# Attention then experts: the first expert's w2 is split on ScalarE and VectorE, piece by piece among the last weighted sums, instead of on GpSimd

## The chip, the cores and the metric

The kernel runs on one core of a Trainium2 chip. The metric is device time in microseconds, from runs of the whole program; lower is better. The core has a matrix engine (TensorE, PE in the rows, PEld for its weight loads), VectorE (DVE), ScalarE (ACT), GpSimd (POOL) and SyncE (SP), which here only issues DMAs. Each engine works through its own instructions in order and waits on semaphores for the others.

## The reference

Attention over 4 batches of 8 heads with a hash mask, and then a mixture of 8 experts, one expert for each token:

```
mask   = q_bucket[:, :, :, None] == k_bucket[:, :, None, :]
scores = where(mask, scale * q @ k.T, -1e9);  attn = softmax(scores);  attn_out = attn @ v
x      = attn_out as (3072, 512)
e_idx  = argmax(x @ w_gate);  gate_w = softmax(...)[e_idx];  eom = sigmoid(x @ w_output_gate)
out[mask_e] = gate_w * eom * (relu(x[mask_e] @ w1[e]) @ w2[e])
```

Sizes: sequence 768, head 64, model width 512, expert width 1024. Everything is float32.

## The kernel before

**Attention.** Heads are taken in 16 pairs, in steps of one 128-row tile. A step makes scores on PE, takes the minimum on DVE (line 534), the exponential on ACT (542), scales on GpSimd (552), transposes on PE with copies on ACT (563, 564), and adds the weighted sum over v on PE (`weighted`, 574). When half of a pair is summed (`c == NT - 1`), DVE copies it to the tile `ot` (577); `rows` transposes it (586) and SP writes it to x_dram (593).

**Routing.** For each batch, small matmuls and some twenty small DVE instructions choose the expert of every token, its rank there and its gate (lines 603 to 710). For the last batch the last pair's part comes in two halves, `add_pair(0)` and `add_pair(1)`: three small matmuls (628) that read `ot`, and one DVE addition (629). Then `best`, `choose`, `prefix`, `gates`, `ranks`, `cols`, `hot`, `table` and `entries` follow.

**The first expert begins early.** The biggest expert is known one batch before the end. Its first 256 tokens are gathered and its w1 is split while attention still runs. Between the pieces of the last routing `fill(f)` issues one eighth of their first layer: 12 matmuls on PE (312), and a ReLU on ACT (322) that writes `hh`. `low()` issues the DVE instruction that goes with an earlier `fill` (323, writes `hl`) and so gives back the bank of PSUM that it used; there are two such banks, so `fill(k)` needs the `low()` of `fill(k-2)`.

**Splitting weights.** Products of float32 are made of three products of rounded parts. A piece of w2 is 128x1024 numbers, 512 KB: `load_weights` loads it into `w_raw`, `split_weights` makes the rounded part (`w2h`, line 175 on GpSimd or 177 on ACT) and the rest (`w2l`, line 178 on GpSimd or on DVE). The first expert has four pieces, f = 0, 2, 4 and 6. There are two `w_raw` buffers at this time, so the load of piece 4 can start only when both instructions on piece 0 are done, and that of piece 6 when those on piece 2 are.

**What sets the order.** PE, DVE, ACT and GpSimd run in the order in which the code between `with tc.manual_schedule` issues their instructions. SP is not among them: its order comes from the planner of the compiler, which takes a DMA when it takes its inputs and its buffer to be ready. In the kernel before, it puts the loads of w2 ahead of writes to x_dram that stand earlier in the code.

After this stretch come the second layer of the first 256 tokens (`down_rows`, ps_s from w2h, w2l), the order of the experts, and the experts one after another.

Of the kernel before, what the change touches and what calls it, by code (L numbers as in the profile page):

```python
# [46 lines left out]
NFB = F // P  # L47
# [12 lines left out]
def lsh_attention_then_moe(  # L60
# [27 lines left out]
    def signed():  # L88

        for h, s in ((0, 1.0), (1, -1.0)):  # L90
            hs = slice(h * D, (h + 1) * D)
            c = 2 * NB * h
            nc.gpsimd.tensor_scalar(pjc[hs, c:c + NB], pj[hs, 0:NB], s, 0.0, ALU.mult, ALU.add)
            nc.gpsimd.tensor_scalar(pjc[hs, c + NB:c + 2 * NB], pj[hs, 0:NB], -s, 0.0, ALU.mult, ALU.add)
# [64 lines left out]
    def load_weights(shape, src):  # L159
        raws.append(len(raws) % 4 if expert[1:] else len(raws) % 2)  # L160
        if raws[-1] < 2:
            raw = wpool.tile(shape, F32, name="w_raw", bufs=2)
        else:

            raw = f32(gp.tile([P, NCC, CAP0], F32R, name=("xh0", "xlo0")[raws[-1] - 2])).rearrange("p a b -> p (a b)")
            if len(shape) == 3:
                raw = raw.rearrange("p (a b) -> p a b", a=shape[1])
        nc.sync.dma_start(raw, src)
        return raw

    def split_weights(pool, tag, bufs, shape, raw, idle=""):
        hi = pool.tile(shape, F32R, name=tag + "h", bufs=bufs)
        lo = pool.tile(shape, F32R, name=tag + "l", bufs=bufs)
        if "h" in idle:
            nc.gpsimd.tensor_scalar(hi, raw, 1.0, 0.0, ALU.mult, ALU.add)
        else:
            nc.scalar.copy(hi, raw)
        (nc.gpsimd if "l" in idle else nc.vector).tensor_tensor(lo, raw, f32(hi), ALU.subtract)  # L178
        return hi, lo
# [10 lines left out]
    def w2_piece(pool, r, f, idle=""):  # L190
        raw = load_weights([P, 2, DM], w2[bass.ds(expert[r], 1), :, f:f + 2].rearrange("e p f d -> p (e f) d"))
        hi, lo = split_weights(pool, "w2", NFB // 2, [P, 2, DM], raw, idle)
        return [(hi[:, j], lo[:, j]) for j in range(2)]
# [108 lines left out]
    def new_h():  # L302
        return [ep.tile([P, NFB, CAP], F32R, name=n) for n in ("hh", "hl")]
# [64 lines left out]
    with ExitStack() as actx:  # L368
# [20 lines left out]
        def load(g, heads=(0, 1)):  # L389
            st = pairs[g]  # L390
            st.setdefault("qk", [])
            for j in heads:
                t = hp.tile([P, S], F32, name="qk", bufs=4)
                nc.sync.dma_start(t, qkT[2 * g + j])
                st["qk"].append(t)

        def load_v(g):
            pairs[g]["v"] = tp.tile([P, 2, NT, D], F32, name="vt", bufs=2)
            nc.sync.dma_start(pairs[g]["v"], v[g])
# [71 lines left out]
        def first_low():  # L471

            st = pairs[0]
            xl, yl, xr, qk = st["xl"][1], st["yl"][1], st["xr"][1], st["qk"][1]
            for n in range(2):
                cs = slice(n * HS, (n + 1) * HS)
                nc.vector.scalar_tensor_tensor(xr[D:P, cs], qk[D:P, cs], 1.0, f32(xl[D:P, cs]), ALU.mult, ALU.subtract)
                nc.vector.scalar_tensor_tensor(yl[0:D, cs], qk[0:D, cs], -0.125, f32(xl[0:D, cs]), ALU.mult,
                                               ALU.subtract)
            nc.gpsimd.tensor_scalar(xl[D:P], qk[0:D], -0.125, 0.0, ALU.mult, ALU.add)  # L480
# [41 lines left out]
        def scores(s):  # L522
            g, hf, t, j = tile_of(s)
            st = pairs[g]
            qs = slice(t * P, (t + 1) * P)
            ss = ps_s.tile([P, 2, 512], F32, name="ps_s")
            kb = D + 2 * NB
            for l, r, k, first in ((st["xl"][j], st["xr"][j], P, True), (st["yl"][j], st["yr"][j], kb, False)):
                for n in range(2):
                    nc.tensor.matmul(ss[:, n, 0:HS], l[0:k, qs], r[0:k, n * HS:(n + 1) * HS],  # L530
                                     start=first, stop=not first)
            sc = tp.tile([P, 2, HS], F32, name="sc", bufs=LAG + 2)
            mn = sp.tile([P, 1], F32, name="mn")
            nc.vector.tensor_scalar(sc, ss[:, :, 0:HS], MASKED, None, ALU.min, ALU.min, accum_out=mn)  # L534
            return sc, mn
# [10 lines left out]
        def normal(s0):  # L546

            rs = sums.pop(s0 // GROUP)
            nc.vector.tensor_scalar(rs, rs, 1e-9, None, ALU.add)
            nc.vector.reciprocal(rs, rs)  # L550
            for k in range(GROUP):
                nc.gpsimd.tensor_scalar(live[s0 + k], live[s0 + k], rs[:, k:k + 1], 0.0, ALU.mult, ALU.add)  # L552
# [26 lines left out]
        def rows(g, hf, whole=True):  # L579

            b, i = divmod(g, H // 2)
            st = pairs[g]
            if hf == 0:
                st["xb"] = gp.tile([P, S // 32, 32], F32, name="xb", bufs=2)
            ts = slice(hf * HS // 32, (hf + 1) * HS // 32)
            nc.vector.transpose(st["xb"][:, ts].rearrange("p n c -> p (n c)"), st["ot"][:, hf * HS:(hf + 1) * HS])
            if whole:
                if hf == 0:
                    return
                ts = slice(0, S // 32)  # L590
            xv = x_dram[b * S:(b + 1) * S].rearrange("(n r) c -> r n c", r=32)
            for a in range(4):
                nc.sync.dma_start(xv[:, ts, i * P + 32 * a:i * P + 32 * (a + 1)], st["xb"][32 * a:32 * (a + 1), ts])
# [246 lines left out]
        with tc.manual_schedule(engines=MANUAL):  # L840
            load(0)
            load(1)
            load_v(0)
            make_identity(nc, ident)

            warm = ps_t.tile([P, 3, P], F32, name="ps_t")
            for i in range(NWARM):
                nc.tensor.transpose(warm[:, i % 3], ident, ident)
            first_heads()
            live = {}  # L850
            for s0 in range(0, NSTEP + LAG, GROUP):
                for s in range(s0, s0 + GROUP):
                    if s < NSTEP:
                        live[s] = scores(s)
                    if s == 0:
                        first_low()
                        signed()
                    if s == s0 and 0 <= s - GROUP < NSTEP:
                        normal(s - GROUP)
                    if 0 <= s - LAG < NSTEP:  # L860
                        transposed(s - LAG, live.pop(s - LAG))
                    if s < NSTEP:
                        live[s] = soft(s, *live[s])
                    for fn in at.get(s, ()):
                        fn()
                for s in range(s0, s0 + GROUP):
                    for fn in products.get(s, ()):
                        fn()


            hctx.close()
            ep = ctx.enter_context(tc.tile_pool(name="ep", bufs=1, side="right", reuse_waits="tile"))
            hs = new_h()
            w2s = []
            lows = []

            def fill(f):
                lows.append(up(early["w1"], early["x"], hs, [f], CAP0))

            def low():  # L880
                lows.pop(0)()

            fill(0)
            for f in range(0, NFB, 2):
                w2s += w2_piece(ep, 0, f, "hl")
            for c in range(NT):
                weighted(2 * NP - 1, c)
                if c == 0:
                    rows(NP - 1, 0, False)
                if c == 2:  # L890
                    r["add_pair"](0, lp)
            fill(1)
            low()
            r["add_pair"](1, lp)
            fill(2)
            r["best"]()
            low()
            r["choose"]()
            rows(NP - 1, 1, False)
            fill(3)  # L900
            low()
            r["prefix"]()
            fill(4)
            r["gates"]()
            low()
            r["ranks"]()
            fill(5)
            low()
            fill(6)
            r["cols"]()  # L910
            low()
            fill(7)
            r["hot"]()
            r["table"]()
            low()
            r["entries"]()
            gid0 = lead_slots(EARLY)
            low()

    mp = ctx.enter_context(tc.tile_pool(name="mp", bufs=1, reuse_waits="tile"))  # L920
    with tc.manual_schedule(engines=MANUAL):
# [17 lines left out]
        for r in range(E):  # L939
# [3 lines left out]
            if r:  # L943
                hs = new_h()
                w2s = []
# [93 lines left out]
    with tc.If(nr > 0):  # L1039
# [12 lines left out]
        with tc.For_i(0, nr, 1):  # L1052
# [13 lines left out]
            for r in range(E):  # L1066
                more = nc.values_load(left[0:1, r:r + 1], min_val=0, max_val=NTOK)
                with tc.If(more > 0):
                    w1s = [w1_piece(wpool, r, cc) for cc in range(NCC)]
                    w2s = []  # L1070
# [53 lines left out]
```

## Time and profile before

| | |
|---|---|
| time, median of 3 runs | 795.59 us (793.64 to 795.8) |
| profiled execution, its own time | 795.53 us |
| its span, first to last instruction | 793.8 us |
| mean granted TensorE clock | 0.990 |
| busy: PE, DVE, ACT, GpSimd | 771.9, 479.1, 458.6, 381.2 us |

Busy times are averages over stages that have different limits; what a change in one stage is worth is read from that stage. Times in the rows below are in microseconds from the start of the span.

### The profile page before, as it was taken

What the parts mean: (1) busy time and instruction counts of PE and PEld (TensorE: products, weight loads), DVE (VectorE), ACT (ScalarE), POOL (GpSimd) and SP (SyncE); (2) the same over time, 40 slices, a digit from 0 to 9 for tenths busy, and PEclk for the clock granted to TensorE, in tenths of its full rate; (3) what the DMA queues carried; (4) which work ended last, traced back from release to release, by engine and by line L of the source; (5) the groups of instructions that cost most, each with busy time, mean ns of one, the idle gap of its engine ahead of it and who ended that gap; (6) DMA issues with size and microseconds to landing.
All of it is one profiled execution on the core that took longest, in us unless ns stands there. A gap on an engine that the chain in (4) does not pass through costs nothing. (4 is left out here: it accounts for less than half of the span.)

```text
span 793.8 us, 13687 instructions
## 1 busy us (share of the span) xinstructions
PE 771.9 (97%) x4674; PEld 607.3 (77%) x4674; DVE 479.1 (60%) x1034; ACT 458.6 (58%) x934; POOL 381.2 (48%) x422
## 2 busy tenths in 40 slices
PE   7999999999999999999999998989999999998997
PEld 4776776677766767676767667978999999988895
DVE  5776666797766796675896737236262635454540
ACT  5877787777777777777768721233252534442331
POOL 6556544444453444544445883462537364645201
PEclk7999999999999999999999999999999999999999
DMA  4563554464564455455456153353444444535501
GB/s 159 128 149 73 115 126 88 110 140 88 122 146 119 87 130 141 90 123 130 88 124 166 56 134 99 92 198 118 143 148 153 149 146 154 176 122 197 195 24 38
DMA packets 84799, 98.88 MB, mean 125 GB/s; under 512 B 57999, under 2 KB 59439, under 8 KB 84720
## 3 DMA queue, kind: packets, MB, share of 16 engines
q1 hardware_dynamic: 79376, 84.58, 40.7%
q0 software_dynamic: 5200, 13.31, 5.2%
q8 instruction: 39, 0.64, 0.3%
q14 instruction: 40, 0.33, 0.1%
q10 hardware_dynamic: 144, 0.02, 0.0%
HBM read 59.49 MB, written 13.11 MB: 91 GB/s over the span
## 5 line engine op out<-in xcount | busy, mean ns | idle before, releaser
L552 POOL TENSOR_SCALAR sc<-sc,rsum 128x768 f32<-128x768 f32 x192 | 179.0, 944 | 219.2 <-DVE rsum L550 88.6
L534 DVE TENSOR_SCALAR_CACHE_REDUCE sc<-ps_s 128x768 f32<-128x768 f32 x192 | 183.3, 955 | 98.1 <-PE ps_s L530 90.1
L564 ACT COPY pts<-ps_t 128x384 f32<-128x384 f32 x384 | 164.6, 482 | 96.8 <-PE ps_t L563 96.3
L542 ACT ACTIVATE sc<-sc,mn 128x768 f32<-128x768 f32 x192 | 181.5, 945 | 15.9 <-DVE sc L534 15.4
L563 PE MATMUL ps_t<-ident,sc 128*128 128x128 f32 x1152 | 158.4, 273 | 3.7 <-ACT pts L564 1.6
L563 PEld LDWEIGHTS ps_t<-ident,sc 128*128 128x128 f32 x1152 | 137.1, 141 | 14.4 <-POOL sc L552 4.0
L574 PE MATMUL ps_a<-pts,vt 128*64 128x384 f32 x768 | 144.8, 499 | 0.0
L530 PE MATMUL ps_s<-xr,xl 128*128 128x384 f32 x384 | 117.9, 388 | 1.9 <-DVE sc L534 1.8
L530 PEld LDWEIGHTS ps_s<-xr,xl 128*128 128x128 f32 x384 | 58.3, 192 | 72.7 <-issue 33.6
L312 PE MATMUL ps_s<-xh,w1h 128*128 128x256 f32 (+7 forms) x288 | 97.9, 340 | 5.2 <-DVE hl L323 4.0
L530 PE MATMUL ps_s<-yr,yl 76*128 76x384 f32 x384 | 100.9, 344 | 1.5 <-POOL yr L439 1.3
L323 DVE SCALAR_TENSOR_TENSOR hl<-ps_s,hh 128x256 fp32r<-128x256 f32 (+8 forms) x40 | 34.0, 849 | 108.8 <-ACT hh L322 97.2
L312 PE MATMUL ps_s<-xh,w1l 128*128 128x256 f32 (+7 forms) x288 | 96.1, 334 | 0.8 <-DVE w1l L178 0.8
L312 PE MATMUL ps_s<-xlo,w1h 128*128 128x256 f32 (+7 forms) x288 | 95.9, 333 | 0.0
L286 POOL DMA_INDIRECT xq<-x_dram,idx x75 | 81.8, 1091 | 21.6 <-issue 21.1
L329 POOL DMA_INDIRECT out_dram<-yo,sid x29 | 30.6, 1056 | 119.6 <-ACT yo L328 73.0
L574 PEld LDWEIGHTS ps_a<-pts,vt 128*64 128x64 f32 x768 | 46.6, 136 | 50.5 <-issue 47.7
L322 ACT ACTIVATE hh<-ps_s 128x256 fp32r<-128x256 f32 (+8 forms) x40 | 29.1, 727 | 94.6 <-PE ps_s L312 81.4
L530 PEld LDWEIGHTS ps_s<-yr,yl 76*128 76x128 f32 x384 | 70.8, 192 | 2.1 <-POOL yr L439 2.1
L312 PEld LDWEIGHTS ps_s<-xh,w1h 128*128 128x128 f32 x288 | 54.7, 190 | 8.7 <-DVE hl L323 4.8
L312 PEld LDWEIGHTS ps_s<-xh,w1l 128*128 128x128 f32 x288 | 54.6, 190 | 2.6 <-DVE w1l L178 1.6
L312 PEld LDWEIGHTS ps_s<-xlo,w1h 128*128 128x128 f32 x288 | 54.6, 190 | 1.1
(204 smaller groups left out, 1017.7 us busy)
## 6 DMA issues: line engine op xcount, KB each, us to landing
w_raw<-in_w_dram SPq DMA_DIRECT2D x36, 512.0 KB
qk<-in_qkT_dram SPq DMA_DIRECT2D x32, 384.0 KB
xh<-in_w_dram SPq DMA_DIRECT2D x14, 512.0 KB
xlo<-in_w_dram SPq DMA_DIRECT2D x14, 512.0 KB
vt<-in_v_dram SPq DMA_DIRECT2D x16, 384.0 KB
xr<-xl SPq DMA_DIRECT2D x30, 192.0 KB
yr<-xl SPq DMA_DIRECT2D x30, 192.0 KB
xr<-yl SPq DMA_DIRECT2D x30, 192.0 KB
```

The lines of the kernel that those rows point to most:

```text
L286: nc.gpsimd.indirect_dma_start(out=xq[:, k * P:(k + 1) * P], out_offset=None, in_=x_dram.rearrange("n (a f) -> (n a) f", a=NB32), in_offse ...
L312: nc.tensor.matmul(ps, l, r, start=first and k == 0, stop=last and k == len(pairs) - 1)
L322: nc.scalar.activation(hh, ph, AF.Relu)
L323: return lambda: nc.vector.scalar_tensor_tensor(hl, ph, 0.0, f32(hh), ALU.max, ALU.subtract)
L329: nc.gpsimd.indirect_dma_start(out=out[:, :], out_offset=bass.IndirectOffsetOnAxis(ap=sid[0:n, r, a:a + 1], axis=0), in_=yo[0:n], in_offse ...
L530: nc.tensor.matmul(ss[:, n, 0:HS], l[0:k, qs], r[0:k, n * HS:(n + 1) * HS], start=first, stop=not first)
L534: nc.vector.tensor_scalar(sc, ss[:, :, 0:HS], MASKED, None, ALU.min, ALU.min, accum_out=mn)
L542: nc.scalar.activation(pr, pr, AF.Exp, bias=mn, scale=-1.0, accum_out=sums[s // GROUP][:, k:k + 1])
L552: nc.gpsimd.tensor_scalar(live[s0 + k], live[s0 + k], rs[:, k:k + 1], 0.0, ALU.mult, ALU.add)
L563: nc.tensor.transpose(tr[:, c], pr[:, (3 * h + c) * P:(3 * h + c + 1) * P], ident)
L564: nc.scalar.copy(pts[:, 3 * h:3 * h + 3, t * P:(t + 1) * P], tr)
L574: nc.tensor.matmul(st["av"][j * D:(j + 1) * D], st["v"][:, j, c], blocks[hb][j][:, c], start=(c == 0), stop=(c == NT - 1))
```

## The change

The loop that issued all four splits on GpSimd ahead of the last weighted sums is gone. The four pieces are now issued one at a time at four places of the same stretch, and without the argument "hl", so that `split_weights` takes ACT for w2h and DVE for w2l. Piece 0 stands where the loop stood; piece 2 behind the first weighted sum and the `rows` there; piece 4 behind the third and its `add_pair(0)`; piece 6 between `add_pair(1)` and `fill(2)`.

```
             fill(0)
-            for f in range(0, NFB, 2):
-                w2s += w2_piece(ep, 0, f, "hl")
+            w2s += w2_piece(ep, 0, 0)
             for c in range(NT):
                 weighted(2 * NP - 1, c)
                 if c == 0:
                     rows(NP - 1, 0, False)
+                    w2s += w2_piece(ep, 0, 2)
                 if c == 2:
                     r["add_pair"](0, lp)
+                    w2s += w2_piece(ep, 0, 4)
             fill(1)
             low()
             r["add_pair"](1, lp)
+            w2s += w2_piece(ep, 0, 6)
             fill(2)
             r["best"]()
             low()
```

## Rows read from the trace of the kernel before

**Rows 1.** The profile's page: busy times of the engines, and the granted TensorE clock in 40 equal slices of the span, in tenths.

```profile
PE 771.9 (97%) x4674; PEld 607.3 (77%) x4674; DVE 479.1 (60%) x1034; ACT 458.6 (58%) x934; POOL 381.2 (48%) x422
PEclk7999999999999999999999999999999999999999
```

**Rows 2.** Busy time by windows of 1 us beside the last routing: window, its length, busy time of PE, PEld, DVE, ACT and POOL with counts, granted clock, DMA share, GB/s.

```profile
477.00:478.00 1.00, 0.62 (x11) 0.52 (x8) 1.00 (x4) 0.39 (x1) 1.00 (x1) 1.00 0.00 0
479.00:480.00 1.00, 0.21 (x2) 0.02 (x1) 0.93 (x8) 0.38 (x1) 0.00 (x0) 1.00 0.65 94
```

**Rows 3.** Timeline of GpSimd: start, duration, engine and line, what it does; in brackets the idle time before it and what ended it. The four pairs of L175 and L178 are the pieces 0, 2, 4 and 6.

```profile
463.80 2.38 POOL L178 TENSOR_TENSOR w2l<-w_raw,w2h 128x1024 fp32r<-128x1024 f32 x1
...
470.30 1.05 POOL L175 TENSOR_SCALAR w2h<-w_raw 128x1024 fp32r<-128x1024 f32 x1 [0.66 <-PE ps_m L628]
...
475.41 1.05 POOL L175 TENSOR_SCALAR w2h<-w_raw 128x1024 fp32r<-128x1024 f32 x1 [1.59 <-DMA w_raw<-in_w_dram]
476.55 2.44 POOL L178 TENSOR_TENSOR w2l<-w_raw,w2h 128x1024 fp32r<-128x1024 f32 x1
488.27 1.38 POOL L254 DMA_INDIRECT xg<-x_dram,gid  x1 [9.29 <-DVE gid L782]
```

**Rows 4.** Timeline of PE: the last matmul of `fill(1)`, and the first ones of `fill(4)` and `fill(5)`.

```profile
473.24 0.28 PE L312 MATMUL ps_s<-xh,w1l 128*128 128x256 f32 x1
...
477.58 0.39 PE L312 MATMUL ps_s<-xh,w1h 128*128 128x256 f32 x1 [0.38 <-DVE hl L323]
...
480.31 0.39 PE L312 MATMUL ps_s<-xh,w1h 128*128 128x256 f32 x1 [1.09 <-DVE hl L323]
```

**Rows 5.** Timeline of VectorE in the same stretch, from the copy of the last pair's first half.

```profile
465.39 0.56 DVE L577 COPY ot<-ps_a 128x384 f32<-128x384 f32 x1 [6.49 <-PE ps_a L574]
465.99 0.58 DVE L586 STREAM_TRANSPOSE xb<-ot 128x384 f32<-128x384 f32 x1
469.86 0.20 DVE L629 TENSOR_TENSOR lgt<-lgt,ps_m 128x48 f32<-128x48 f32 x1 [3.30 <-PE ps_m L628]
471.96 0.56 DVE L577 COPY ot<-ps_a 128x384 f32<-128x384 f32 x1 [1.89 <-PE ps_a L574]
...
474.15 0.20 DVE L629 TENSOR_TENSOR lgt<-lgt,ps_m 128x48 f32<-128x48 f32 x1 [1.30 <-PE ps_m L628]
...
475.30 0.21 DVE L645 TENSOR_TENSOR eq<-eq,expi 128x48 f32<-128x48 f32 x1
...
475.78 0.74 DVE L648 TENSOR_TENSOR oneh<-ei,expi 128x48 f32<-128x48 f32 x1
...
477.56 1.50 DVE L656 TENSOR_TENSOR en<-en,oneh 128x48 f32<-128x48 f32 x1
...
479.84 0.42 DVE L323 SCALAR_TENSOR_TENSOR hl<-ps_s,hh 128x256 fp32r<-128x256 f32 x1
```

**Rows 6.** Timeline of ScalarE in the same stretch: the ReLUs of `fill(0)`, `fill(1)` and `fill(2)`, and the instruction behind the last.

```profile
466.99 0.38 ACT L322 ACTIVATE hh<-ps_s 128x256 fp32r<-128x256 f32 x1 [2.56 <-PE ps_s L312]
473.56 0.38 ACT L322 ACTIVATE hh<-ps_s 128x256 fp32r<-128x256 f32 x1 [6.18 <-PE ps_s L312]
475.64 0.38 ACT L322 ACTIVATE hh<-ps_s 128x256 fp32r<-128x256 f32 x1 [1.70 <-PE ps_s L312]
475.92 0.23 ACT L638 ACTIVATE ex<-df 128x48 f32<-128x48 f32 x1
```

**Rows 7.** Timeline of SP's queue: the loads of pieces 2 and 4 (in one row: start of the first, time to the end of the second), piece 4 alone, the first writes of the last pair's first half to x_dram, and the load of piece 6.

```profile
460.94 5.62 SPq L168 DMA_DIRECT2D w_raw<-in_w_dram  x2
466.20 0.36 SPq L168 DMA_DIRECT2D w_raw<-in_w_dram  x1
466.61 0.94 SPq L593 DMA_DIRECT2D x_dram<-xb  x2
469.66 0.36 SPq L168 DMA_DIRECT2D w_raw<-in_w_dram  x1
```

**Rows 8.** Splits of later experts on ACT and DVE: one pair in the timelines, then the durations of all from whole pieces in `w_raw` (minimum/median/maximum in ns, first and last start).

```profile
539.85 1.04 ACT L177 CAST w2h<-xh 128x1024 fp32r<-128x1024 f32 x1
541.03 1.21 DVE L178 TENSOR_TENSOR w2l<-xh,w2h 128x1024 fp32r<-128x1024 f32 x1
L178 DVE TENSOR_TENSOR w2l<-w_raw,w2h x14: 1215/1220/1226, 536.0 to 762.5; 128x1024 fp32r<-128x1024 f32 x14
```

**Rows 9.** PE around 730 us, behind a wait, in the timeline; and by windows (columns as in rows 2) that stretch and two near the start of the span.

```profile
726.20 0.33 PE L312 MATMUL ps_s<-xlo,w1h 128*128 128x368 f32 x1
726.37 0.33 PE L312 MATMUL ps_s<-xh,w1l 128*128 128x368 f32 x1
729.20 0.43 PE L312 MATMUL ps_s<-xh,w1h 128*128 128x368 f32 x1 [2.50 <-DVE hl L323]
...
731.05 0.51 PE L312 MATMUL ps_s<-xh,w1h 128*128 128x368 f32 x1
731.36 0.51 PE L312 MATMUL ps_s<-xlo,w1h 128*128 128x368 f32 x1
...
10.86:14.27 3.41, 1.93 (x5) 1.14 (x4) 3.32 (x7) 1.03 (x2) 2.28 (x3) 0.50 0.00 0
14.27:17.69 3.42, 3.04 (x13) 1.40 (x13) 2.41 (x8) 2.33 (x5) 2.35 (x7) 0.50 0.35 115
730.87:734.28 3.41, 3.41 (x14) 3.41 (x13) 3.41 (x4) 1.76 (x2) 1.00 (x1) 0.55 0.73 234
```

More of the change, by code (lines that the diff above doesn't have):

```diff
@@ L883, in lsh_attention_then_moe @@
             fill(0)
-            for f in range(0, NFB, 2):
-                w2s += w2_piece(ep, 0, f, "hl")
+            w2s += w2_piece(ep, 0, 0)
             for c in range(NT):
@@ L889, in lsh_attention_then_moe @@
                     rows(NP - 1, 0, False)
+                    w2s += w2_piece(ep, 0, 2)
                 if c == 2:
                     r["add_pair"](0, lp)
+                    w2s += w2_piece(ep, 0, 4)
             fill(1)
@@ L894, in lsh_attention_then_moe @@
             r["add_pair"](1, lp)
+            w2s += w2_piece(ep, 0, 6)
             fill(2)
```

## The prediction

> **What bounds the kernel now.** I read the page first. PE is busy for 97% of the span and its granted clock is nearly full all the way [rows 1], so the end moves by whatever time PE gains or loses. Next I read one-microsecond windows around the last routing, because PE is not full there: 0.62 us busy in the window from 477 and 0.21 us in the one from 479, while VectorE is full in the first and 0.93 in the second [rows 2]. Then I read the timelines of the five queues over the same stretch. PE's gaps end with VectorE's L323, the `low()` that gives a PSUM bank back: 0.38 us before `fill(4)` and 1.09 us before `fill(5)` [rows 4]. So in this stage VectorE's chain decides: from `add_pair(1)` through `best`, `choose` and `gates` to the L323 at 479.84.
>
> Two links of that chain are longer than their kind. The 128x48 two-input form takes 0.21 us (L645); L648 takes 0.74 and L656 takes 1.50 [rows 5]. Both run beside a GpSimd split and end with it: L648 at 476.52, w2h at 475.41 + 1.05 = 476.46; L656 at 479.06, w2l at 476.55 + 2.44 = 478.99 [rows 3, 5]. GpSimd thus costs the chain 0.53 + 1.29 = 1.82 us. That is all the change can hand back here; GpSimd's next work is the gather at 488.27, which waits for VectorE and not for the splits [rows 3].
>
> **The change, part by part.**
>
> **Taken away:** 1.82 us of VectorE's waits, as above.
>
> **Added on ScalarE and VectorE:** four times 1.04 and 1.22 us [rows 8]. Both are idle for most of 467 to 473: ScalarE for 6.18 us before the ReLU of `fill(1)` [rows 6], and VectorE between 466.57 and 471.96 but for one 0.20 us addition [rows 5]. So the work is there to hide. The question is when the data come, since each new instruction waits in order and holds up what stands behind it. I follow them one by one.
>
> Piece 0. ScalarE takes w2h behind the ReLU of `fill(0)`, which starts at 466.99 when `fill(0)` is done on PE [rows 6]. ScalarE starts its next instruction 0.28 us after a ReLU's start (475.64, 475.92) [rows 6]: 467.27 to 468.31. VectorE follows 0.15 us later (cast end 540.88, subtraction 541.03) [rows 8]: 468.46 to 469.68.
>
> Piece 2. SP issued its load at 460.94 [rows 7], before anything that the change touches, and I expect the same again, so the data are there. w2h ends at 469.3. On VectorE the transpose of `rows` stands ahead of w2l and behind piece 0, so it moves from 465.99 to about 469.65 and its x_dram writes from 466.61 to 470.2 [rows 5, 7]; nobody needs these before the gather at 488.27, so the 18 us until then hide the move. w2l runs from 470.2 to 471.4.
>
> Piece 4 is the one that matters. Its load needs piece 0's buffer. Before, SP issued it at 466.20, when GpSimd's w2l of piece 0 was done (463.80 + 2.38 = 466.18) [rows 3, 7]. Now that is 469.70. GpSimd started on the landed piece at 470.30, 4.10 us after the issue; for piece 6 it was 475.41 - 469.66 = 5.75 us [rows 3, 7]. These are the two bounds. I take 4.10, as here too two x_dram writes follow the load: data at 473.8, w2h to 474.85, w2l from 475.0 to 476.2.
>
> What is queued behind: on ScalarE the ReLU of `fill(1)`, from 473.56 to about 474.8. On VectorE the copy L577 of the last half, before at 471.96 [rows 5], then the `low()` of `fill(0)`. L577 now runs from 476.15 to 476.7. `add_pair(1)` reads `ot`, so PE's next step after `fill(1)`, whose last matmul starts at 473.24 [rows 4], begins at 476.75 instead of right there: 3.5 us later. PE works in order and `fill(2)` needs the bank that the `low()` behind L577 gives back, so nothing fills the gap.
>
> Piece 6. Its buffer comes free at 471.4; the load lands between 475.5 and 477.2 by the same two bounds, w2h ends at 476.6 to 478.2. On VectorE w2l stands behind the addition L629, now due at 477.7 to 477.9, and ahead of `best`: 1.22 us in the chain, and 0 to 0.5 us of wait. I take no wait. From L629 to the L323 of 479.84 VectorE has next to no idle time before [rows 5], so these 1.22 us add in full and the 1.82 us come off in full.
>
> So `fill(5)` begins 3.5 - 1.8 + 1.2 = 2.9 us later than 480.31. What follows on PE and for the gather hangs on the same chain and moves along. SP's later loads do too. Nothing later gives the time back, as PE is full.
>
> **The clock.** PE would stand still for some 3.3 us between 473.5 and 476.75. Elsewhere a wait of 2.50 us before 729.20 was followed by a granted clock of 0.55 from 730.87 to 734.28 [rows 9], that is nearly all at the 1.2 GHz level. There the 368-column matmuls start 0.31 us apart, against 0.17 at 2.4 GHz [rows 9]; eleven of them cost 0.14 x 11 = 1.5 us. Here `fill(2)` would end in a wait of about 1.1 us for the L323 behind piece 6's w2l, which swallows part. I take 1.0 us; the bounds are 0 (no fall) and 3.5 us (three such stretches, 4.6, less 1.1: near the start the clock stayed at 0.50 in two windows in a row [rows 9]).
>
> The Trainium skill ("TensorE: Matmul & The Clock Gate", What's actually happening) says that the half clock is the default state and that activity releases it. By that rule a kernel that trades short VectorE waits for one long PE wait pays twice. The trace agrees around 730 us; without it the sum would be 2.9, with it 3.9.
>
> **Sum:** + 3.5 - 1.8 + 1.2 + 1.0 = + 3.9 us on the profiled execution's own 795.53, which lies 0.06 below the median of the runs. Forecast 799.5.
>
> **The rivals.**
>
> **Not slower: the wait is hidden and the contention is what counts.** The 1.82 us come back and the new work fits into idle time. It decides if piece 4's w2l is done when L577 is due. Without any wait for data it would run from about 471.6 to 472.85, L577 would end at 473.4 and `add_pair(1)` come 0.2 us late: 0.2 - 1.8 + 1.2 = - 0.4 us, or 795.1; were piece 6 hidden too, - 1.6 us, or 793.9. For it: both engines are half idle. Against it: the load would have to be issued by 467.5, and its buffer is in use until 469.7. The Trainium skill ("SBUF — State Buffer", Who interferes with whom) has VectorE and GpSimd lock each other out of a shared port pair for a whole instruction; read alone, it makes this change a gain, of the size of this rival. Even all 1.82 us are under 0.3% (2.4 us), about what a measurement of this kernel can tell from no change.
>
> **Slower by more: SP's order.** SP is ordered by the planner; before, two writes to x_dram stood between loads that precede them all in the code [rows 7]. If it put the four writes of `rows` (0.47 us each [rows 7]) ahead of piece 2's load, that would be issued at 472.1 and land at 476.2; w2h, w2l of piece 2 (478.6), w2l of piece 4 (479.8), L577: `add_pair(1)` at 480.4, + 7.1 - 0.6 + 1.5 for the clock = + 8, or 803.5. Against it: piece 2's load went out at 460.94 [rows 7], when its buffer was free, and the writes have no data before 466.57, in the new order 470.2. A load of piece 4 that straggles as piece 6's did (+ 1.65) or more clock (+ 2.5) leads to 801 to 803 in a milder way.
>
> **The same: a smaller wait.** If the clock does not fall and one of the small terms (handovers, an idle spot in the chain that takes the w2l of piece 6) is 0.6 us better, the sum is under 2.4 us: 797.5.
>
> **How the numbers follow.** The stall at `add_pair(1)`, with 2.4 to 6 us in all: 0.70. More than that (SP's order, stragglers, clock): 0.10. The same by a smaller wait or a hidden one: 0.17. Faster by over 0.3%: 0.03, as it needs more than the contention. So slower 0.80, same 0.17, faster 0.03. For the range: the main case without the clock and with 0.4 us less is 798.0; I go to 797.2 to take in the smaller wait. At the top 3.9 + 1.65 leads to 801.1, with part of the clock's bound to 802.5. It leaves the SP order and most of the hidden wait outside.
>
> **What would show it.** In the changed profile: w2h on ScalarE at about 467.3 and SP's load of piece 4 at 469.7; ScalarE's w2h of piece 4 ended by a DMA at about 473.8; VectorE's L577 of the last half at 476 instead of 471.96; PE idle for 3 to 3.6 us before L628; L648 and L656 at 0.2 us; a granted clock below 1 somewhere in 475 to 485. The prediction is wrong if L577 still comes near 472 to 473.5, if SP's loads stand in another order, or if PE has other work in the gap.

## The result: 0.9% slower, and the profile after

The changed kernel takes 803.53 us, median of 4 runs (802.1 to 803.96), where the kernel before, run beside it, takes 795.69 (793.64 to 796.91). The ratio is 1.0092, with a 95% interval of 1.0072 to 1.0112: about 7.3 us more, 5.7 to 8.9. The forecast was 799.5, with a range of 797.2 to 802.5. Sign and place were right; the size was not. The profiled execution took 803.96 us, its span 802.2 us (before 793.8), its mean granted clock is 0.983 (before 0.990).

The page of the changed kernel, its busy times and the granted clock in 40 slices, to be held against [rows 1]:

```profile
PE 774.6 (97%) x4674; PEld 610.4 (76%) x4674; DVE 481.3 (60%) x1038; ACT 462.1 (58%) x938; POOL 367.3 (46%) x414
PEclk7999999999999999999999999999999999999999
```

GpSimd lost eight instructions and 13.9 us, ScalarE and VectorE got four each and 3.5 and 2.2 us. PE does the same 4674 matmuls, busy for 2.7 us more; the span grew by 8.4. The rest of the loss, 5.7 us, is therefore time in which PE stands still, and the timeline of PE in the changed kernel has it in one row. (The row says 7.12; the waits of 0.38 and 1.09 us before `fill(4)` and `fill(5)` [rows 4] are gone.)

```profile
473.06 0.28 PE L312 MATMUL ps_s<-xh,w1l 128*128 128x256 f32 x1
480.46 1.49 PE L628 MATMUL ps_m<-wgt,ot 128*128 128x32 f32 x6 [7.12 <-DVE ot L577]
481.76 0.56 PE L312 MATMUL ps_s<-xh,w1h 128*128 128x256 f32 x1
482.12 0.41 PE L312 MATMUL ps_s<-xlo,w1h 128*128 128x256 f32 x1
482.33 0.41 PE L312 MATMUL ps_s<-xh,w1l 128*128 128x256 f32 x1
...
493.61 0.47 PE L312 MATMUL ps_s<-w2h,hh 128*128 128x512 f32 x1
```

The first row is the last matmul of `fill(1)` [rows 4]. Then `add_pair(1)` waits 7.12 us for VectorE's copy L577. The `fill` matmuls behind the wait come to start 0.21 us apart; at full clock they start 0.11 to 0.12 apart. The last row is the first product of the second layer, which ends this stage. The same two places in the kernel before, PE's start of `add_pair(1)` and its first product of the second layer:

```profile
473.36 0.75 PE L628 MATMUL ps_m<-wgt,ot 128*128 128x32 f32 x6
...
486.21 0.47 PE L312 MATMUL ps_s<-w2h,hh 128*128 128x512 f32 x1
```

Upstream, VectorE's timeline of the changed kernel, the counterpart of [rows 5]:

```profile
468.20 1.23 DVE L178 TENSOR_TENSOR w2l<-w_raw,w2h 128x1024 fp32r<-128x1024 f32 x1 [2.39 <-ACT w2h L177]
469.35 0.57 DVE L586 STREAM_TRANSPOSE xb<-ot 128x384 f32<-128x384 f32 x1
469.84 1.18 DVE L178 TENSOR_TENSOR w2l<-w_raw,w2h 128x1024 fp32r<-128x1024 f32 x1
...
478.71 1.22 DVE L178 TENSOR_TENSOR w2l<-w_raw,w2h 128x1024 fp32r<-128x1024 f32 x1 [7.57 <-ACT w2h L177]
479.86 0.55 DVE L577 COPY ot<-ps_a 128x384 f32<-128x384 f32 x1
481.98 0.20 DVE L629 TENSOR_TENSOR lgt<-lgt,ps_m 128x48 f32<-128x48 f32 x1 [1.25 <-PE ps_m L628]
482.11 1.22 DVE L178 TENSOR_TENSOR w2l<-w_raw,w2h 128x1024 fp32r<-128x1024 f32 x1
...
484.62 0.21 DVE L648 TENSOR_TENSOR oneh<-ei,expi 128x48 f32<-128x48 f32 x1
485.87 0.19 DVE L656 TENSOR_TENSOR en<-en,oneh 128x48 f32<-128x48 f32 x1
```

The four w2l are those of pieces 0, 2, 4 and 6. The third stands ahead of L577 and waits 7.57 us for ScalarE; the fourth stands in the chain behind L629. L648 and L656, which took 0.74 and 1.50 us beside GpSimd's splits [rows 5], are down to 0.21 and 0.19.

ScalarE's timeline, the counterpart of [rows 6], says what piece 4 waits for:

```profile
467.14 1.98 ACT L177 CAST w2h<-w_raw 128x1024 fp32r<-128x1024 f32 x2
477.64 1.04 ACT L177 CAST w2h<-w_raw 128x1024 fp32r<-128x1024 f32 x1 [8.52 <-DMA w_raw<-in_w_dram]
478.59 0.38 ACT L322 ACTIVATE hh<-ps_s 128x256 fp32r<-128x256 f32 x1
```

And SP's queue, the counterpart of [rows 7], says why its load is late:

```profile
460.81 0.36 SPq L168 DMA_DIRECT2D w_raw<-in_w_dram  x1
469.95 3.28 SPq L593 DMA_DIRECT2D x_dram<-xb  x4
473.47 0.98 SPq L168 DMA_DIRECT2D w_raw<-in_w_dram  x2
485.56 1.89 SPq L593 DMA_DIRECT2D x_dram<-xb  x4
```

Before, the order on SP was: load of piece 4, two writes to x_dram, load of piece 6, six writes. Now it is: four writes, load of piece 4, load of piece 6, four writes. Piece 0's buffer is free at 468.20 + 1.23 = 469.43. The writes need the transpose, done at 469.35 + 0.57 = 469.92, and take 3.28 us to issue. So the load goes out at 473.47, four microseconds after its buffer was free, and ScalarE starts on the piece 4.17 us later.

While PE waits, its clock falls, as the window of 6.80 us from 478.30 shows (columns as in rows 2; PEclk 0.50 is the 1.2 GHz level):

```profile
478.30:485.10 6.80, 4.64 (x21) 4.64 (x22) 4.97 (x14) 2.06 (x5) 0.00 (x0) 0.50 0.00 1
```

**Where the 8.4 us of span went.** I split the span at the two PE rows: the start of `add_pair(1)` (473.36 before, 480.46 after) and the first product of the second layer (486.21, 493.61). Up to the first: + 7.1. Between the two, which I call the stage below: 12.85 before, 13.15 after, + 0.3. From there to the end: 307.6 before, 308.6 after, + 1.0. The last term I don't put down to the change: the experiments below show the same kernel with 300.7 and 307.7 in two executions.

### The profile page after: what moved, and what is told of

The parts are those of the page before. It is cut to its first block, busy times and chain, and to the rows that moved or that the text cites. A ratio compares the mean times of both kernels' runs of the same rounds, so it can differ in the third digit from the quotient of the medians.

```text
span 802.2 us, 13679 instructions
## 1 busy us (share of the span) xinstructions
PE 774.6 (97%) x4674; PEld 610.4 (76%) x4674; DVE 481.3 (60%) x1038; ACT 462.1 (58%) x938; POOL 367.3 (46%) x414
```

## The experiments

They ran in three groups, each with its own runs of the kernel before (medians 796.42, 793.05 and 792.6 us), so kernels are compared by their ratio to the kernel before of their own group. The ratios and intervals are those on record; they are not the quotient of two medians, which would be 1.0099 for the changed kernel and 1.0063 for e1. The lengths of the stage come from the single profiled execution of each.

**What the order on SP costs.** In e1 `rows` only transposes and returns its four writes as a function, which is called behind the load of piece 4; all else is the changed kernel.

```
                 if c == 0:
-                    rows(NP - 1, 0, False)
+                    write = rows(NP - 1, 0, False, True)
                     w2s += w2_piece(ep, 0, 2)
                 if c == 2:
                     r["add_pair"](0, lp)
                     w2s += w2_piece(ep, 0, 4)
+                    write()
```

> The changed kernel, but the four writes of the last pair's first half to x_dram are issued behind piece 4, so that SP sends the load of piece 4 ahead of them. Theory (the loss is one wait of PE at add_pair(1) for the load of piece 4, and SP's order made it longer): the load goes out at about 469.6 instead of 473.47, L577 of the last half starts at about 476 instead of 479.86, PE waits some 3.3 us instead of 7.12, and the time is about 799.7 us (803.5 less 3.8), which is also what my forecast had without the planner's order. Rival (the splits lengthen the chain by their own 1.04 and 1.22 us on ScalarE and VectorE, whatever the loads do): no change, 803.5. Second rival (a lower clock behind the wait is the larger part): PE's wait is shorter but the clock still falls, and the time falls by less than 2 us.

Measured: ratio 1.0049 (1.0033 to 1.0066), + 3.9 us, where the changed kernel has 1.0092. By these ratios the order is a little under half of the loss; in the traces it takes PE's wait from 7.12 to 5.01 us. Its SP queue, then ScalarE's and PE's rows for piece 4 and `add_pair(1)`:

```profile
469.54 0.36 SPq L168 DMA_DIRECT2D w_raw<-in_w_dram  x1
470.03 2.04 SPq L595 DMA_DIRECT2D x_dram<-xb  x4
```

```profile
475.61 1.04 ACT L177 CAST w2h<-w_raw 128x1024 fp32r<-128x1024 f32 x1 [6.40 <-DMA w_raw<-in_w_dram]
```

```profile
478.43 1.49 PE L634 MATMUL ps_m<-wgt,ot 128*128 128x32 f32 x6 [5.01 <-DVE ot L577]
```

The load goes out at 469.54, where the prediction had 469.70. But it takes 6.07 us until ScalarE starts, not 4.10, more than the upper bound of 5.75. The wait is 5.01 us, not 3.3, and the stage takes 13.25. So the agreement of + 3.9 us with the forecast's sum is partly luck: in the trace the wait alone is 1.5 above the sum's 3.5. The profiled execution took 804.04 us, the longest of the kernel's four (the others 800.59 to 801.56), and its time behind the stage is 310.5, 3 more than before's.

**Whether the writes slow the load.** In e8 the transpose and the writes of that half move behind `choose`, so that the loads of pieces 4 and 6 have SP to themselves.

```
                 if c == 0:
-                    rows(NP - 1, 0, False)
                     w2s += w2_piece(ep, 0, 2)
...
             r["choose"]()
+            rows(NP - 1, 0, False)
             rows(NP - 1, 1, False)
```

> The changed kernel, but the transpose and the four writes of the last pair's first half stand behind choose, so that the loads of pieces 4 and 6 have SP and the DMA engines to themselves. In the run with the writes behind piece 4 the load took 6.1 us to land, where my forecast had 4.1. Theory (the small writes behind it slow the load): piece 4's load goes out at about 469.6, ScalarE starts on it 4.1 us later, PE waits 3.0 to 3.5 us at add_pair(1), and the time is about 1.5 us less than with the writes right behind the load, 3 us over the kernel before (0.5 us of it the transpose, which now stands in the chain). Rival (the load takes 6 us anyway, as ScalarE's and VectorE's new work or chance slows it): 4 us or more over the kernel before.

Measured: ratio 1.0042 (1.0027 to 1.0057), + 3.3 us. SP and ScalarE:

```profile
469.07 1.47 SPq L168 DMA_DIRECT2D w_raw<-in_w_dram  x2
```

```profile
474.72 1.04 ACT L177 CAST w2h<-w_raw 128x1024 fp32r<-128x1024 f32 x1 [5.99 <-DMA w_raw<-in_w_dram]
```

Issued at 469.07, used at 474.72: 5.65 us with no write beside it, and PE waits 4.55 us, not 3.0 to 3.5. So in the trace the theory that the small writes make the load long falls. That the time agrees with the theory's 3 us is luck: the stage takes 13.34, and the part behind it is short in this execution (303.9). What goes with the long loads is one line in the view of the DMA queues, in the stretch of the load (queue, kind, packets, MB, share of 16 engines):

```profile
q8 instruction: 1, 0.02, 1.0%
```

It is there in e8 (469.07 to 475) and in e1 (469.54 to 475.7), and also with the load that gave the prediction its upper bound, that of piece 6 before (469.66 to 475.41, 5.75 us). In the stretches of the two short loads, before (466.2 to 470.2) and after (473.47 to 478), there is none. In the three long ones 15 of 16 parts had landed by 3.8 to 4.3 us and the last by 5.6 to 6.0. But e9, the kernel before once more, has the packet too while piece 6 is loaded, and there the load took 4.63 us. So the packet alone does not make a load long. That it can hold up one engine's part is a guess: no run made it come or go.

**What the clock costs.** e4 gives PE work in the gap: 50 transposes of the identity, whose result nobody uses.

```
             low()
+            warm = ps_t.tile([P, 3, P], F32, name="ps_t")
+            for i in range(50):
+                nc.tensor.transpose(warm[:, i % 3], ident, ident)
             r["add_pair"](1, lp)
```

> The changed kernel, with 50 more transposes of the identity on PE in the gap ahead of add_pair(1), about 6 of its 7.1 us; their result is not used. Theory (the lower clock behind the gap costs about 1 us by itself): the granted clock stays at 1.00 from 473 to 490, the matmuls of fill(2) start 0.12 us apart instead of 0.21, and the time is 802.3 us (1 to 1.5 under 803.5). Rival (the clock's fall is hidden, as VectorE's chain decides there): clock full and time unchanged within 0.4 us. Second rival (the clock is most of the loss): 799 or less.

Measured: ratio 1.0055 (1.003 to 1.0081). The five times reach from 799.4 to 803.0, so the ratio settles little; their median, 799.91, is nearer to the second rival's 799 than to the theory's 802.3. The trace says more: in its PE timeline the gap is filled and `add_pair(1)` comes at the same time as in the changed kernel, 480.43; the window over it has the clock at 1.00.

```profile
473.43 5.62 PE L897 MATMUL ps_t<-ident 128*128 128x128 f32 x50
480.43 0.85 PE L628 MATMUL ps_m<-wgt,ot 128*128 128x32 f32 x6 [1.37 <-DVE ot L577]
```

```profile
473.30:480.40 7.10, 5.75 (x53) 5.51 (x51) 1.72 (x3) 2.32 (x3) 0.00 (x0) 1.00 0.52 155
```

From there the stage takes 12.12 us instead of 13.15. The fall of the clock thus costs 1.0 us in the stage, in what is a gap of 7 us. That is the theory's 1 us. The rest of e4's gain lies behind the stage (305.1), where its kernel does not differ from the changed one.

**Whether the contention comes back.** e2 takes the wait away and leaves the splits where the change put them: pieces 4 and 6 get buffers of their own and are loaded early.

```
+            own = [w2_load(0, f, True) for f in (4, 6)]
             for c in range(NT):
...
-                    w2s += w2_piece(ep, 0, 4)
+                    w2s += w2_piece(ep, 0, 4, raw=own[0])
...
-            w2s += w2_piece(ep, 0, 6)
+            w2s += w2_piece(ep, 0, 6, raw=own[1])
```

> The changed kernel, but pieces 4 and 6 have two buffers of their own and their loads are issued right behind piece 0, so that nothing has to wait for a buffer. The splits stay where the change put them, on ScalarE and VectorE. Theory: with the data there, piece 4's w2l ends at about 473, add_pair(1) comes 0.2 us late at most, L648 and L656 take 0.2 us, the clock stays full, and the time is 0.4 us under the kernel before, 795.3 (794 to 796.2). Rival (the splits' own time lengthens the chain): a wait of 2 us or more at add_pair(1) stays and the time is 798 or more.

Measured: ratio 0.9974 (0.996 to 0.9987), 2.1 us faster than before. In VectorE's timeline (L653 and L661 are L648 and L656 of the kernel before):

```profile
472.40 0.55 DVE L582 COPY ot<-ps_a 128x384 f32<-128x384 f32 x1
...
474.22 0.20 DVE L634 TENSOR_TENSOR lgt<-lgt,ps_m 128x48 f32<-128x48 f32 x1 [0.94 <-PE ps_m L633]
474.98 1.23 DVE L180 TENSOR_TENSOR w2l<-w_own,w2h 128x1024 fp32r<-128x1024 f32 x1 [0.56 <-ACT w2h L179]
...
477.51 0.21 DVE L653 TENSOR_TENSOR oneh<-ei,expi 128x48 f32<-128x48 f32 x1
...
478.76 0.20 DVE L661 TENSOR_TENSOR en<-en,oneh 128x48 f32<-128x48 f32 x1
```

With the data in time the copy to `ot` is at 472.40, `add_pair(1)` at 473.43 and no wait is left there: the whole stall came from the late load of piece 4, which had waited for its buffer and for the writes. The stage is 12.69, hardly below 12.85, and the rows say why: the 1.82 us come back, but piece 6's w2l takes 0.56 + 1.23 = 1.79 of the same chain. So the stage explains little of the 2.1 us (the theory had 0.4), and the profiled execution shows none of it: its span is 793.8 us, as before. A second execution in the next group, e2b, is the same kernel:

> The kernel of the run with own buffers on ScalarE and VectorE, once more, beside the two others with own buffers: about 1.5 us under the kernel before, 0.9974 of its time, or between 0.996 and 0.9987 as its interval said.

Measured: 0.9968 (0.9953 to 0.9984), stage 12.68. Behind the stage it takes 300.7 us, the first one 307.7: so much does that part vary between executions of one kernel.

**The contention without the work in the chain.** e3 moves the splits of pieces 4 and 6 to the end of the routing.

```
                     r["add_pair"](0, lp)
-                    w2s += w2_piece(ep, 0, 4)
...
             r["add_pair"](1, lp)
-            w2s += w2_piece(ep, 0, 6)
...
             r["table"]()
             low()
+            w2s += w2_piece(ep, 0, 4)
             r["entries"]()
             gid0 = lead_slots(EARLY)
             low()
+            w2s += w2_piece(ep, 0, 6)
```

> The changed kernel, but piece 4 is split behind the table and piece 6 behind the last slots, out of the way of add_pair(1) and of best. Theory: no wait at add_pair(1), no split beside the chain, no GpSimd beside it: the 1.8 us of contention come off in full and nothing is added, 793.9 us (793.3 to 795). Rival (the second layer's first products then wait for w2l of pieces 4 and 6): PE waits at f = 4 or 6 and the time is 796 or more.

Measured: ratio 1.0033 (1.0014 to 1.0052), slower, where the theory had a gain. Half of it held: the stage takes 11.02 us, 1.83 less than before, just the 1.82 of the prediction. The other half was not foreseen. VectorE, GpSimd and PE:

```profile
487.47 1.21 DVE L178 TENSOR_TENSOR w2l<-w_raw,w2h 128x1024 fp32r<-128x1024 f32 x1
```

```profile
487.49 2.51 POOL L254 DMA_INDIRECT xg<-x_dram,gid  x1 [24.89 <-DVE gid L782]
```

```profile
495.40 1.13 PE L266 MATMUL ps_t<-ident,xg 128*128 128x128 f32 x4 [3.87 <-DMA xg<-x_dram,gid]
```

The gather that feeds the next expert runs beside piece 6's w2l and takes 2.51 us instead of 1.38 [rows 3]. Its first rows are used 7.91 us after it started; before, the same transpose followed without a wait, 4.97 us after its gather, as PE's row shows:

```profile
493.24 0.63 PE L266 MATMUL ps_t<-ident,xg 128*128 128x128 f32 x4
```

In e3 PE waits 3.87 us, and the granted clock is 0.62 in the window from 494.10 to 497.50. So the gain was given back at the next thing that hung on VectorE and GpSimd. Of the 2.94 us of delay 1.13 are the longer gather; how much of the rest is the weight loads that go out beside it (SP issues two at 488.17) was not taken apart.

**Who should split.** e6 is the kernel before with the early buffers alone, all four pieces on GpSimd. e7 shares: pieces 0 and 2 on GpSimd, 4 and 6 on ScalarE and VectorE from the early buffers, both ahead of `add_pair(1)`.

```
# e6
+            own = [w2_load(0, f, True) for f in (4, 6)]
             for f in range(0, NFB, 2):
-                w2s += w2_piece(ep, 0, f, "hl")
+                w2s += w2_piece(ep, 0, f, "hl", own[f // 2 - 2] if f > 2 else None)
# e7
+            own = [w2_load(0, f, True) for f in (4, 6)]
+            for f in (0, 2):
+                w2s += w2_piece(ep, 0, f, "hl")
+            w2s += w2_piece(ep, 0, 4, raw=own[0])
...
                     rows(NP - 1, 0, False)
+                    w2s += w2_piece(ep, 0, 6, raw=own[1])
```

> The kernel before, with GpSimd making all four splits, but pieces 4 and 6 have buffers of their own and are loaded early. It tells whether what the run with own buffers on ScalarE and VectorE gained came from the engines or from the buffers. Theory (the engines: VectorE's two-input instructions wait while GpSimd splits): GpSimd now works without gaps from 462.6 to about 476.6, so piece 6 still stands beside choose; one VectorE instruction there waits about 1.2 us instead of two that wait 1.8, and the time is 0.6 us under the kernel before (0.2 to 1.2). Rival (early loads are the gain): as fast as the run with own buffers on ScalarE and VectorE, 1.5 us or more under the kernel before.

> Own, early loaded buffers for pieces 4 and 6 as there; GpSimd splits pieces 0 and 2, which it ends at about 469.6, and ScalarE and VectorE split 4 and 6 behind fill(0) and behind the first weighted sum. Theory: all splits are over by 472.6, no split and no GpSimd instruction stands beside best, choose and gates, add_pair(1) comes on time within 0.3 us, and from add_pair(1) to the second layer's first product it takes 11.0 us, as where pieces 4 and 6 were split late, instead of 12.85. Time 1.8 us under the kernel before, somewhat under the run with own buffers. Rival (VectorE's subtraction of piece 4 waits for GpSimd's of piece 2 and L577 comes over 1 us late): no faster than the run with own buffers.

Measured: e6 0.9977 (0.9965 to 0.9989), e7 0.997 (0.9959 to 0.9981). e6's 1.8 us are more than its theory's 0.6 and meet its rival, that early loads are the gain. Yet its stage is 12.81, as before: the early buffers don't take the contention away, they move it. One VectorE instruction waits in place of two, and for as long (1.99 - 0.21 = 1.78 us, not the theory's 1.2). In VectorE's and GpSimd's timelines:

```profile
474.55 1.99 DVE L641 TENSOR_TENSOR df<-lgt,mx 128x48 f32<-128x48 f32 x1
```

```profile
474.12 2.37 POOL L180 TENSOR_TENSOR w2l<-w_own,w2h 128x1024 fp32r<-128x1024 f32 x1
```

e7's stage is 11.44, 1.4 below before. There the contention falls on an instruction of VectorE that has room: piece 4's w2l, 2.36 us instead of 1.23, beside GpSimd's w2l, and the copy to `ot` still comes at 472.38.

```profile
468.38 2.36 DVE L180 TENSOR_TENSOR w2l<-w_own,w2h 128x1024 fp32r<-128x1024 f32 x1 [2.40 <-ACT w2h L179]
...
472.38 0.54 DVE L582 COPY ot<-ps_a 128x384 f32<-128x384 f32 x1
```

**Is e6's gain real?** Its chain is not shorter, so I ran it once more, together with e7's kernel (e11) and the kernel before under another label (e9), to see what a comparison of a kernel with itself gives.

> The kernel before, timed against itself: the ratio should be 1.000 and its interval shows how small a difference these comparisons can tell (I expect plus or minus 0.0015). Its trace shows whether the waits of PE behind the second layer (0.5 to 1.2 us near 528, 2.5 us near 729 and the clock's fall behind it) belong to the kernel or change from one execution or chip to the next: theory, they change, by 3 us or more of the stretch from the second layer's first product to the end (307.6 us in the first trace).

> The kernel before with own, early loaded buffers for pieces 4 and 6, all splits on GpSimd, once more. Its stretch from add_pair(1) to the second layer's first product took 12.81 us against 12.85, yet it was timed at 0.9977 of the kernel before. Theory (the ratio came from the later waits, which are not its own): 1.000, or between 0.998 and 1.001. Rival (something in it does save time): again 0.9965 to 0.9989.

> The kernel with GpSimd on pieces 0 and 2 and ScalarE and VectorE on pieces 4 and 6, own buffers, once more. Its stretch from add_pair(1) to the second layer's first product took 11.44 us against 12.85. Theory: that 1.4 us is kept to the end, 0.998 of the kernel before (0.9965 to 0.9992). Rival (the later waits take it back): 1.000 within 0.001.

Measured: e9 1.0006 (0.9992 to 1.002), e10 0.9975 (0.9964 to 0.9986), e11 0.9963 (0.995 to 0.9976). So a kernel held against itself comes out within 0.2%. e6's gain repeats in its rival's range, with a stage of 12.84 in e10; a ratio of 1.000 is outside the interval. e11's ratio is a little under its own range; its stage is 11.43. Behind the stage e9 takes 304.7 us against 307.6 in the first execution, 2.9 where its theory had 3 or more; the wait near 729 is there again (2.65 us), the waits near 528 are not.

A hint on e6 is in e9's trace, an execution of the kernel before whose stage took 14.78 us. Piece 6 landed sooner there, so GpSimd split it from 474.29 on and not from 475.41, beside other instructions of VectorE. VectorE's timeline, then GpSimd's:

```profile
474.65 0.74 DVE L636 TENSOR_TENSOR df<-lgt,mx 128x48 f32<-128x48 f32 x1
...
475.65 2.20 DVE L644 TENSOR_SCALAR eq<-df 128x48 f32<-128x48 f32 x1
```

```profile
474.29 1.05 POOL L175 TENSOR_SCALAR w2h<-w_raw 128x1024 fp32r<-128x1024 f32 x1 [0.34 <-DMA w_raw<-in_w_dram]
475.43 2.38 POOL L178 TENSOR_TENSOR w2l<-w_raw,w2h 128x1024 fp32r<-128x1024 f32 x1
```

In the first execution, without a split beside them, these two took 0.21 and 0.18 us. So the contention costs 0.53 + 2.02 = 2.55 us here and not 1.82, and it is not only two-input instructions that wait: L644 has one input. Its PE rows and its windows from 477 and 480.5:

```profile
478.86 0.20 PE L675 MATMUL ps_m<-ohb,tri 128*128 128x48 bf16 x1 [1.33 <-DVE ohb L651]
479.65 0.39 PE L312 MATMUL ps_s<-xh,w1h 128*128 128x256 f32 x1 [0.44 <-DVE hl L323]
```

```profile
477.00:480.40 3.40, 1.63 (x18) 1.32 (x17) 3.23 (x14) 0.38 (x1) 0.81 (x1) 1.00 0.06 9
480.50:483.90 3.40, 3.40 (x18) 3.40 (x18) 2.92 (x17) 0.38 (x1) 0.00 (x0) 0.50 0.32 47
```

PE is 1.63 us busy of 3.40, and the clock is at 0.50 in the window behind; the other execution of the kernel before kept 1.00 and took 12.85. Of the 1.93 us between the two stages 0.73 are contention; the other 1.2 come behind it, where the clock is low. e10 has the same windows like this:

```profile
477.00:480.40 3.40, 3.26 (x31) 3.24 (x32) 3.16 (x18) 0.45 (x2) 0.00 (x0) 1.00 0.20 29
480.50:483.90 3.40, 3.37 (x29) 3.17 (x28) 3.33 (x17) 1.15 (x3) 0.00 (x0) 1.00 0.19 29
```

In e6 and e10 GpSimd's split of piece 6 waits for no load, and it stood beside the same instruction in both executions (L641, 1.99 and 2.04 us). One of two executions of the kernel before had the fall, and none of the six with early buffers, whose windows from 477 to 483.9 all have 1.00. If it comes in about half of the executions it is worth some 1 us on average, half of e6's gain; that is an argument, not a proof, and the other half stays open. e11, at 789.38 us beside 792.6, has the lowest ratio, 0.37% under the kernel before (0.24 to 0.5%); the intervals of e10 and e2b overlap its own.

## Why the prediction was right and wrong

**The place: right.** PE was to wait before `add_pair(1)`, behind L577, behind piece 4's w2l, behind its load. Each link stands in the rows after, and e2 shows the reverse: with piece 4 in time the wait is gone, and with it the whole loss.

**SP's order: the step that failed.** The prediction dated the load of piece 4 by its buffer alone: SP had issued it before when GpSimd's w2l of piece 0 was done, and "now that is 469.70". Measured 473.47, + 3.8 us: the buffer was free at 469.43, but SP sent the four writes first.

The text knew that the planner orders SP, named another order of the loads among the signs of being wrong, and made it a rival that shared 0.10 of the chances with stragglers and the clock. Its time, 803.5, is what was measured, but that is luck. I had put the writes ahead of piece 2's load. That one went out at 460.81, as I had argued, and the writes went ahead of piece 4's instead, where I had not looked.

Two things on record pointed there. In the kernel before, all four loads stand ahead of these writes in the code; the change puts those of pieces 2, 4 and 6 behind them. e1, which puts the writes behind piece 4 again, gets that load first. And by the prediction's own times the buffer (469.70) and the writes' data (470.2) come free half a microsecond apart, as they did (469.43 and 469.92). Why the planner then chose the writes is not on record. Each write took 0.82 us to issue, too, not the 0.47 of [rows 7]; in e1, e3 and e4 it was 0.51 to 0.68. A near tie in a queue that I don't order should have had a chance near one half, with its price, four writes of 0.5 to 0.8 us or 2 to 3.3 us, inside the range.

**The stall: + 7.1 instead of + 3.5,** in this execution by that step alone: with the load at 473.47, the prediction's own sum (4.10 for the load, casts, copy) gives 480.5, and 480.46 is measured. e1 shows that the load's length was a second gap: 6.07 us there, outside both bounds. Two rows of before were too few to bound a transfer: the same load of piece 6 took 5.75 us in one execution of the kernel before and 4.63 in the other (e9).

**The contention: right.** - 1.82 forecast; L648 and L656 fell by 0.53 and 1.31 us, and e3's stage by 1.83.

**Piece 6's w2l in the chain: right for the change,** 1.22 us with no wait (482.11). In e2, where its load is early, it is 1.79, as there it waits 0.56 us for ScalarE's w2h.

**The clock: right, its size in part by luck.** 1.0 forecast, for a wait of 3.3 us and eleven slow matmuls; 1.0 by e4, but behind a wait of 7.1 us, with the clock at 0.50 for 6.8. The stage of the changed kernel adds up: 12.85 - 1.82 + 1.22 + 1.0 = 13.25, measured 13.15. The rule of the Trainium skill ("TensorE: Matmul & The Clock Gate", What's actually happening), that PE goes at half clock unless activity releases it, agrees: 0.50 behind the idle gap, 1.00 with the gap filled in e4.

**Nothing later gives it back: right.** Behind the stage the changed kernel took 1.0 us more, within what one kernel shows.

**The rival that the contention is what counts** named a real gain, and its rule (the Trainium skill, "SBUF — State Buffer", Who interferes with whom) holds here, in one more place than I used: in e7 it is VectorE's instruction that takes 2.36 us instead of 1.23 beside GpSimd's. But a term of 1.8 us could not decide beside a load that is late by several. Its condition was also worked out too mildly: for a w2l from 471.6 on, the load's 4.10 us and the cast's 1.04 + 0.15 need an issue by 466.3, not 467.5.

## What to carry to other kernels

Before moving work to an engine whose queue has a critical instruction behind the new place, find when its input's buffer comes free, which DMAs now stand ahead of its load in the code, and what the queue will issue first at that moment; if two are free within a microsecond, price both orders. Where memory allows, give the moved data a buffer of its own and load it early: here that turned a loss of 0.9% into a gain of about 0.3%. And count what contention gives back against the work put into the same chain: 1.82 came back and 1.79 went in.

## What the hardware showed that I had not expected

- A 512 KB load took 4.10 to 6.07 us from issue to use, and the same load of the same kernel 5.75 and 4.63 in two executions. In the three longest (5.65, 5.75, 6.07) one sixteenth of it came 1.4 us or more after the rest. Of the nine followed in these traces, the five longer ones (4.63, 5.21, 5.65, 5.75, 6.07) had one 16 KB packet of instructions in their stretch, the four shorter ones (4.10, 4.17, 4.24, 4.48) none; no run tested it.
- GpSimd's indirect gather took 0.96 to 0.98 us in the traces where no two-input instruction of VectorE was running when it began; 1.37 or 1.38 in nine traces, the kernel before among them, where one of 0.6 us had just begun; and 2.51 in e3, where a w2l of 1.21 had. Spans on GpSimd are rough, but the order is the same in all 13 traces.
- In e9 the clock fell to 0.50 behind gaps of 1.33 and 0.44 us, where another execution of the same kernel kept it behind gaps of 0.38 and 1.09 [rows 4]. The stage with the fall is 1.9 us longer, of which 0.7 are contention.
